# Row statistics by ScalarE's summed squares, in a convolution and expert kernel

## The chip, the cores and the metric

The kernel runs on one core of a Trainium2 chip. The metric is the device time of one execution in microseconds (us). A core has TensorE (matmuls into PSUM), VectorE, ScalarE and GpSimd (elementwise work), and SyncE, whose queue issues most DMA transfers. In the profile they are PE (PEld is its loading of weights), DVE, ACT, POOL and SP. Each runs its instructions in program order and waits on semaphores for the others.

## What is computed

The reference, cut to what matters; S = 2048 rows, D = 512 columns, 8 experts with F = 1792:

```python
def _A_ref(q, k, v, shift_k, ssm_k, ssm_D):
    k_shift = ...                      # causal depthwise convolution of 4 taps
    kv = k_shift * v
    y = irfft2(rfft2(kv_pad) * rfft2(kf_pad))[:S]   # causal convolution over all S rows
    y = y + kv * ssm_D
    return q * y

def _B_ref(x, w_gate, w1, w2):
    logits = xf @ w_gate
    topk_idx = argsort(-logits)[:, :1]
    gates = softmax(topk_val)
    for e in range(E):
        out = out + w * (silu(xf @ w1[e]) @ w2[e])   # w: gate where topk_idx == e, else 0
    ...

x = A_q
h = x + _A_ref(_layernorm(x), A_k, A_v, A_shift_k, A_ssm_k, A_ssm_D)
h2 = h + _B_ref(_layernorm(h), B_w_gate, B_w1, B_w2)
```

The second layer norm needs, for each row of h, its mean and variance over the 512 columns. They are "the second statistics" of this document. The mean does not enter the logits, since the gate's weights have their column means taken out; the variance scales them, which does not move the largest one.

## The kernel before

**Three stages.** The convolution with all that belongs to h; the routing (which row goes to which expert, and a table of rows); the experts, one after the other, with their weights streamed from memory.

**The convolution.** The 2048 rows lie as 128 partitions x 16, and the columns as 4 channels (`c`) of 128. Four of the 16 make a unit (`u`), so a unit is a tile of 128 x 4 x 128, and with four a channel there are 16. For each channel: ScalarE, GpSimd and VectorE make the taps, TensorE turns them (`turn_kv`), VectorE multiplies by v, and stage A (`stage_a`, eight groups of four matmuls for the kernel and eight for kv, into the two `pa` buffers, copied out by ScalarE as `st`) does the first part of a Fourier transform. The second part runs by half channels, eight in all, numbered `i` from 0 to 7: VectorE transposes (`turn`), TensorE multiplies small blocks (`stage_b`, into the one buffer `pb` of four PSUM banks), ScalarE copies (`keep_u`), VectorE multiplies twice (`product1`, `product2`, each after a further block of stage B), TensorE goes back (`back`), and VectorE transposes back (`unturn`, line 350). From one `unturn` to the next is called a period here; the fifth period ends with the fifth of them.

**What belongs to h.** When both halves of a channel are back, each of its four units goes through `last_stage` (TensorE), `gate` (VectorE), `residual` (GpSimd; VectorE for the last channel), which completes h of that unit and channel. Then TensorE turns the unit (`turn_kv` again, line 277), ScalarE copies it (`keep_h`), and for each pair of units TensorE multiplies it with the gate's weights (`logits`) and VectorE adds the result to one sum, `lacc` (`sum_logits`). VectorE also makes the second statistics: `stats` runs four `bn_stats` a unit and channel, and `aggr`, after the last channel, four `bn_aggr` a unit. SyncE stores h (`store_h`). The logits of four channels are summed this way, so that after the last unit one transpose of `lacc` on TensorE gives the routing its logits.

**The order.** The instructions of the convolution are not written in the order of the text. Steps are added to a `Plan` with an engine, a cost and a due time; `Plan.run` picks for each engine the next step, by what is ready and what is due first, and so writes each engine's queue. The due times come from tables (`DK`, `DG`, `DF` and others). PSUM buffers are handed out in turn: `pa` has 2, `pb` 1, `pm` (turned units and logits) 2.

**The routing.** Maximum of the logits, candidates, ranks by a scan and three small matmuls, a table of rows by 16 small matmuls. Then GpSimd gathers the first expert's rows from memory, where h and its four numbers a row (`rec`: mean, root of the variance, two for the gate) were stored.

Of the kernel before, what the change touches and what calls it, by code (L numbers as in the profile page):

```python
# [16 lines left out]
P = 128  # L17
S, D, F, E, KS = 2048, 512, 1792, 8, 4
NJ = S // P
# [112 lines left out]
def kernel(  # L132
# [17 lines left out]
    lacc = keep.tile([P, P], F32, name="lacc")  # L150
    bst2 = keep.tile([P, NJ, ND, 6], F32, name="bst2")
# [28 lines left out]
    ps = conv.enter_context(tc.tile_pool(name="ps", bufs=1, space=PSUM))  # L180
# [8 lines left out]
    GAP = (NU - 1) * E  # L189
    wgc = cp.tile([P, (GAP + E) * ND + GAP], F32, name="wgc")  # L190
    mv1 = cp.tile([P, 2, NJ], F32, name="mv1")
# [185 lines left out]
    def stats(c, u):  # L377
        for i in range(UJ):
            nc.vector.bn_stats(bst2[:, u * UJ + i, c, :], T["h", c, u][:, i, :])

# [3 lines left out]
    def gate_w(c, u):  # L384
        a = (GAP + E) * c + GAP - E * u
        return wgc[:, a:a + NU * E]

    def logits(c, p):
        pl = pt("pm", ("pl", c, p), [P, P])
        for n, u in enumerate((2 * p, 2 * p + 1)):  # L390
            for j in range(UJ):
                nc.tensor.matmul(pl[32 * j:32 * j + 32, :], gate_w(c, u), T["ht", c, u][:, j, :],
                                 start=n == 0, stop=n == 1)

    def sum_logits(c, p):
        if c == 0 and p == 0:
            nc.vector.tensor_copy(lacc, T["pl", c, p])
        else:
            nc.vector.tensor_add(lacc, T["pl", c, p], lacc)

    def aggr(u):
        for j in range(u * UJ, u * UJ + UJ):
            nc.vector.bn_aggr(rec[:, j, 0:2], bst2[:, j, :, :].rearrange("p c s -> p (c s)"))
# [22 lines left out]
    def wg_less():  # L426
        for c in range(ND):
            a = (GAP + E) * c + GAP
            nc.vector.scalar_tensor_tensor(wgc[:, a:a + E], T["pc"], -1.0 / D, wg_sb[:, c, :],
                                           op0=ALU.mult, op1=ALU.add)  # L430

    def casts():
# [5 lines left out]
        nc.gpsimd.tensor_scalar(tok_b, const("tb"), const("ta"), None, op0=ALU.add)  # L438
# [5 lines left out]
    nc.scalar.activation(mv1[:, 0, 0:1], lacc[:, 0:1], AF.Copy)  # L444
    for _ in range(30):
        nc.tensor.matmul(pt("pa", "warm", [P, P]), lacc,
                         lacc, start=True, stop=True)


    DK = (-2.742, -0.93, -7.553, -1.532, -0.994, -6.403)  # L450
    DA = (-0.515, -0.166, -1.312)

    DG = (-7.756, -9.196, -16.731, -2.007, -8.949, -7.899, -12.936, -15.886, 3.939, 2.112)
# [636 lines left out]
```

## Time and profile before

| | |
|---|---|
| three runs | 549.56, 547.93 and 549.28 us; median 549.28 |
| the profiled execution's own time | 549.0 us |
| its span, first to last instruction | 547.1 us |
| PE busy | 521.2 us (95%) |
| DVE busy | 404.2 us (74%) |
| ACT busy | 264.9 us (48%) |
| POOL busy | 262.3 us (48%) |

A busy share is a mean over three stages with different limits, and so the profile is read by stretches. The convolution takes the first 172 us up to its last `unturn` and some 13 more for the last channel's units; the routing starts at about 185 us, the experts' first matmul is at 201 us, and the rest is the experts. The rows of the trace have the start in us from the span's start, the duration, the engine, the line, and the tile that is written with those that are read; in brackets stands how long the engine had been idle and what ended that.

### The profile page before, as it was taken

The numbers are of one execution on the slowest core, as the hardware profiler recorded it, in microseconds if no ns is written. First come the engines' busy times: TensorE is split into PE (matmuls) and PEld (weight loads), VectorE is DVE, ScalarE is ACT, GpSimd is POOL, SyncE is SP. The second block draws the span as 40 slices with busy tenths as digits, with TensorE's granted clock in tenths as the row PEclk, the third lists the DMA queues.
The fourth block names the chain that finished last, engine by engine and source line by source line (L and its number), as shares of the span: only waits on it lengthen the run. The fifth ranks groups of instructions, "written<-read, shape, count | busy, mean of one in ns | idle before, by whom it ended". The sixth has DMA issues, their size and how long they took to land. (4 is left out here: it accounts for less than half of the span.)

```text
span 547.1 us, 12112 instructions
## 1 busy us (share of the span) xinstructions
PE 521.2 (95%) x4800; PEld 451.8 (83%) x4800; DVE 404.2 (74%) x554; ACT 264.9 (48%) x409; POOL 262.3 (48%) x294
## 2 busy tenths in 40 slices
PE   9999989999988699899999999999999999999994
PEld 9867776777646569689999999999988988988973
DVE  3779898999897968857953793884895784784851
ACT  2787886544220336535534444544553553553520
POOL 0555648975550135707703830850770760851831
PEclk9999999999999879999999999999999999999998
DMA  8946586678641269674554555665567467566401
GB/s 282 384 164 199 182 256 180 187 196 281 185 146 40 61 221 350 231 245 144 182 193 155 200 182 161 219 211 181 194 207 253 156 212 247 191 217 204 153 2 40
DMA packets 42452, 105.26 MB, mean 192 GB/s; under 512 B 6464, under 2 KB 14784, under 8 KB 42002
## 3 DMA queue, kind: packets, MB, share of 16 engines
q1 hardware_dynamic: 39602, 95.89, 52.8%
q0 software_dynamic: 2784, 8.51, 4.8%
q8 instruction: 40, 0.66, 0.5%
q14 instruction: 26, 0.21, 0.1%
HBM read 95.96 MB, written 8.47 MB: 191 GB/s over the span
## 5 line engine op out<-in xcount | busy, mean ns | idle before, releaser
L817 POOL TENSOR_TENSOR hl<-s,hh 128x240 fp32r<-128x240 f32 (+5 forms) x112 | 117.2, 1060 | 162.4 <-DVE hh L816 161.8
L798 DVE TENSOR_TENSOR wlo<-raw,whi 128x1024 fp32r<-128x1024 f32 x112 | 159.7, 1439 | 44.7 <-ACT whi L797 44.6
L797 ACT ACTIVATE whi<-raw 128x1024 fp32r<-128x1024 f32 x112 | 114.7, 1052 | 3.9 <-DMA raw<-in_w_dram 3.9
L815 ACT ACTIVATE s<-acc 128x240 f32<-128x240 f32 (+5 forms) x112 | 43.1, 387 | 107.1 <-PE acc L812 67.3
L816 DVE CAST hh<-s 128x240 fp32r<-128x240 f32 (+5 forms) x112 | 55.1, 502 | 37.6 <-ACT s L815 37.4
L812 PE MATMUL acc<-xh,whi 128*128 128x240 f32 (+5 forms) x448 | 72.7, 284 | 0.6 <-ACT xh L773 0.6
L812 PE MATMUL acc<-xl,whi 128*128 128x240 f32 (+5 forms) x448 | 72.0, 283 | 0.0
L812 PE MATMUL acc<-xh,wlo 128*128 128x240 f32 (+5 forms) x448 | 71.9, 283 | 0.0
L812 PEld LDWEIGHTS acc<-xh,whi 128*128 128x128 f32 x448 | 61.7, 189 | 1.3 <-ACT xh L773 0.8
L812 PEld LDWEIGHTS acc<-xl,whi 128*128 128x128 f32 x448 | 61.5, 189 | 0.0
L812 PEld LDWEIGHTS acc<-xh,wlo 128*128 128x128 f32 x448 | 61.4, 189 | 0.0
L832 PE MATMUL acc<-whi,hh 128*128 128x512 f32 (+2 forms) x140 | 55.9, 399 | 0.0
L832 PE MATMUL acc<-whi,hl 128*128 128x512 f32 (+2 forms) x140 | 55.3, 395 | 0.0
L832 PE MATMUL acc<-wlo,hh 128*128 128x512 f32 (+2 forms) x140 | 55.0, 393 | 0.0
L265 POOL TENSOR_TENSOR acc<-acc,ac 128x512 f32<-128x512 f32 x26 | 33.1, 1279 | 37.5 <-ACT acc L253 19.1
L835 PE MATMUL acc<-hh,whi 128*128 128x304 f32 (+2 forms) x168 | 49.8, 296 | 0.0
L835 PE MATMUL acc<-hl,whi 128*128 128x304 f32 (+2 forms) x168 | 49.2, 293 | 0.0
L835 PE MATMUL acc<-hh,wlo 128*128 128x304 f32 (+2 forms) x168 | 49.2, 293 | 0.0
L296 ACT ACTIVATE st<-pa 128x512 f32<-128x512 f32 x64 | 37.3, 595 | 19.7 <-PE pa L293 19.6
L293 PEld LDWEIGHTS pa<-kv,tw 128*128 128x128 f32 x256 | 30.2, 191 | 12.2 <-ACT st L296 8.7
L293 PE MATMUL pa<-kv,tw 128*128 128x128 f32 x256 | 33.5, 282 | 2.2 <-ACT st L296 2.2
L835 PEld LDWEIGHTS acc<-hh,whi 128*128 128x128 f32 x168 | 31.6, 188 | 0.1
(157 smaller groups left out, 848.1 us busy)
## 6 DMA issues: line engine op xcount, KB each, us to landing
raw<-in_w_dram SPq DMA_DIRECT2D x112, 512.0 KB, 4.2
tv<-in_tab_v_dram SPq DMA_DIRECT2D x12, 512.0 KB, 4.5
h<-in_q_dram SPq DMA_DIRECT2D x16, 256.0 KB, 4.4
kt<-in_kt_dram SPq DMA_DIRECT2D x3, 1216.0 KB, 8.1
v<-in_v_dram SPq DMA_DIRECT2D x12, 256.0 KB, 4.4
kern<-in_ssm_dram SPq DMA_DIRECT2D x12, 256.0 KB, 3.4
h<-in_x_dram SPq DMA_DIRECT2D x12, 256.0 KB, 3.9
h_dram<-h SPq DMA_DIRECT2D x12, 256.0 KB, 3.5
```

The source lines that it names most:

```text
L265: nc.gpsimd.tensor_add(T[a, c, u], T[a, c, u], T[b, c, u])
L293: nc.tensor.matmul(p[:, :, j], tw[:, u * UJ + j, r, :], src[:, j, :], start=True, stop=True)
L296: nc.scalar.activation(T["s" + kind, c][:, r * NU + u], T["pa", kind, c, u, r], AF.Copy)
L797: nc.scalar.activation(whi, raw, AF.Copy)
L798: nc.vector.tensor_sub(wlo, raw, whi.bitcast(F32))
L812: nc.tensor.matmul(pu, a[:, k, fs], b[:, k, :], start=i == 0, stop=i == 3 * ND - 1)
L815: nc.scalar.activation(s, pu, AF.Silu)
L816: nc.vector.tensor_copy(hh[:, f, :], s)
L817: nc.gpsimd.tensor_sub(hl[:, f, :], s, hh[:, f, :].bitcast(F32))
L832: nc.tensor.matmul(pd[:ds_.stop - ds_.start], b[:, f, ds_], a[:, f % 2, :], start=f == 0 and i == 0, stop=f == 2 * NCH - 1 and i == 2)
L835: nc.tensor.matmul(pd, a[:, f % 2, ds_], b[:, f, :], start=f == 0 and i == 0, stop=f == 2 * NCH - 1 and i == 2)
```

## The change

Three things change together.

**The second statistics.** `stats` and `aggr` on VectorE go. In their place ScalarE runs `squares`: for each of the four 128x128 slices of a unit one ACTIVATE `Square` of h minus the first norm's mean (its bias, one number a partition), whose sum over the 128 columns goes to `sq`. The sum of h itself comes out of the logits: the gate's weights get a ninth column of ones, and each unit's logits so have nine columns. For that the weights of a channel now have 32 columns, 16 for each unit of a pair, and `lacc` has two halves, one for each pair of units. After the convolution GpSimd adds the four channels of `sq`, divides, and takes the square of the mean's difference off.

**The last unit.** The last unit of the last channel is turned and copied in two halves (`turn_half`, `keep_half`), and its logits don't pass through `lacc`: four matmuls add them in PSUM to the transposed `lacc`.

**The order.** All tables of due times are new, with a table `DE` of its own for the last channel; in the routing a reciprocal, the exponential and the store of `rec` stand later.

The diff, cut to its core:

```diff
-    lacc = keep.tile([P, P], F32, name="lacc")
-    bst2 = keep.tile([P, NJ, ND, 6], F32, name="bst2")
+    lacc = keep.tile([P, 2, P], F32, name="lacc")
+    sq = keep.tile([P, NJ, ND], F32, name="sq")
...
-    wgc = cp.tile([P, (GAP + E) * ND + GAP], F32, name="wgc")
+    wgc = cp.tile([P, 32 * ND + 16], F32, name="wgc")
+    junk = cp.tile([P, P], BF16, name="junk")
...
-    def stats(c, u):
-        for i in range(UJ):
-            nc.vector.bn_stats(bst2[:, u * UJ + i, c, :], T["h", c, u][:, i, :])
...
+    def turn_half(c, u, k):
+        p = pt("pm", ("pht", c, u, k), [P, 2, P])
+        for i in range(2):
+            nc.tensor.transpose(p[:, i, :], T["h", c, u][:, 2 * k + i, :], ident)
+
+    def keep_half(c, u, k):
+        t = T["ht", c, u] if k else sb("ht", ("ht", c, u))
+        nc.scalar.activation(t[:, 2 * k:2 * k + 2], T["pht", c, u, k], AF.Copy)
+
+    def squares(c, u):
+        for i in range(UJ):
+            j = u * UJ + i
+            nc.scalar.activation(junk, T["h", c, u][:, i, :], AF.Square, bias=mv1[:, 0, j:j + 1],
+                                 accum_out=sq[:, j, c:c + 1])
...
-    DF = (2.156, 4.2, -1.718, -7.172, -11.095, -0.093, -7.929, 1.515, -6.905, 5.228, -10.922)
+    DF = (2.33, 3.001, -2.081, -12.063, -6.5, -3.31, -11.581, -4.654, -5.162, 4.313, -35.62)
+    DE = (2.794, -2.565, -5.315, -14.858, -3.123, 1.353, -8.873, -8.482, 0.765, -0.771, -22.145)
...
-            add("DVE", 0.8, o + DF[9], stats, c, u, uses=[("h", c, u)], makes=[(None, ("bs", c, u))])
-            add("SP", 0.26 * MB, o + DF[10], store_h, c, u, uses=[("h", c, u)])
-            if c == ND - 1:
-                add("DVE", 0.6, o + DF[9] + 0.1, aggr, u, uses=[("bs", k, u) for k in range(ND)])
+            add("ACT", 1.2, o + f[9], squares, c, u, uses=[("h", c, u), "mv1"])
+            add("SP", 0.26 * MB, o + f[10], store_h, c, u, uses=[("h", c, u)])
...
-    nc.tensor.transpose(pl, lacc, ident)
+    nc.tensor.matmul(pl[:, 0], lacc[:, 0], ident, start=True, stop=True)
+    nc.tensor.matmul(pl[:, 1], lacc[:, 1], ident, start=True, stop=False)
+    for j in range(UJ):
+        nc.tensor.matmul(pl[:, 1, 32 * j + 16:32 * j + 17 + E], T["ht", ND - 1, NU - 1][:, j, :],
+                         gate_w(ND - 1, 0)[:, :E + 1], start=False, stop=j == UJ - 1)
...
+    nc.scalar.activation(in_j(rec[:, :, 0]), in_t(plj[:, :, E]), AF.Copy, scale=1.0 / D)
+    nc.gpsimd.tensor_add(sq[:, :, 0:2], sq[:, :, 0:2], sq[:, :, 2:4])
+    nc.gpsimd.tensor_add(var, sq[:, :, 0], sq[:, :, 1])
+    nc.gpsimd.tensor_scalar(var, var, 1.0 / D, EPS, op0=ALU.mult, op1=ALU.add)
+    nc.gpsimd.tensor_add(rec[:, :, 1], rec[:, :, 0], mv1[:, 0, :])
+    nc.gpsimd.tensor_mul(rec[:, :, 1], rec[:, :, 1], rec[:, :, 1])
+    nc.gpsimd.tensor_sub(rec[:, :, 1], var, rec[:, :, 1])
```

VectorE in the eighth period, before (L379 is `bn_stats`, L338 and L342 the products, L318 and L350 the transposes, L369 the gate, L399 the logits' sum):

```order
L350 STREAM_TRANSPOSE zs<-pb 128x64x16x2
L369 TENSOR_TENSOR xn<-pa,xn 128x512
L318 STREAM_TRANSPOSE xa<-st 128x2048
L379 BN_STATS bst_63<-h 128x6 x4
L369 TENSOR_TENSOR xn<-pa,xn 128x512
L338 TENSOR_TENSOR p_2087<-pb,xb 128x2048
L379 BN_STATS bst_63<-h 128x6 x4
L399 TENSOR_TENSOR lacc<-pm,lacc 128x128
L379 BN_STATS bst_63<-h 128x6 x4
L342 TENSOR_TENSOR xb<-pb,xb 128x2048
L369 TENSOR_TENSOR xn<-pa,xn 128x512
L350 STREAM_TRANSPOSE zs<-pb 128x64x16x2
```

VectorE in the same period after the change (L320 and L352 the transposes, L340 and L344 the products, L371 the gate, L395 the logits' sum):

```order
L352 STREAM_TRANSPOSE zs<-pb 128x64x16x2
L395 TENSOR_TENSOR lacc<-pm,lacc 128x128
L371 TENSOR_TENSOR xn<-pa,xn 128x512
L320 STREAM_TRANSPOSE xa<-st 128x2048
L371 TENSOR_TENSOR xn<-pa,xn 128x512
L340 TENSOR_TENSOR p_2087<-pb,xb 128x2048
L395 TENSOR_TENSOR lacc<-pm,lacc 128x128
L344 TENSOR_TENSOR xb<-pb,xb 128x2048
L371 TENSOR_TENSOR xn<-pa,xn 128x512
L352 STREAM_TRANSPOSE zs<-pb 128x64x16x2
```

The statistics are gone from between the products; the three gates stand there as they did, and a second sum of logits has come in.

TensorE in the fifth period, before, from its first block of stage B to the way back (L329 is stage B, and the way back where it reads `p`; L365 the last stage, L293 stage A, L277 the turning of a unit):

```order
L329 MATMUL pb<-xa,cb 32x512 x16
L365 MATMUL pa<-zs,tv 128x128 x8
L293 MATMUL pa<-kv,tw 128x128 x4
L329 MATMUL pb<-xb,cb 32x512 x16
L293 MATMUL pa<-kv,tw 128x128 x4
L277 MATMUL pm<-cs,h 128x128 x4
L277 MATMUL pm<-cs,acc 128x128 x4
L293 MATMUL pa<-kern,tw 128x128 x4
L329 MATMUL pb<-xb,cb 32x512 x16
L293 MATMUL pa<-kv,tw 128x128 x8
L277 MATMUL pm<-cs,h 128x128 x4
L329 MATMUL pb<-p_1458,cb 32x512 x16
```

TensorE there after the change (L331 is stage B and the way back, L367 the last stage, L295 stage A, L279 the turning, L390 the logits):

```order
L331 MATMUL pb<-xa,cb 32x512 x16
L295 MATMUL pa<-kv,tw 128x128 x8
L279 MATMUL pm<-cs,acc 128x128 x4
L331 MATMUL pb<-xb,cb 32x512 x16
L279 MATMUL pm<-cs,h 128x128 x4
L367 MATMUL pa<-zs,tv 128x128 x8
L331 MATMUL pb<-xb,cb 32x512 x16
L390 MATMUL pm<-ht,wgc 32x128 x8
L295 MATMUL pa<-kv,tw 128x128 x8
L331 MATMUL pb<-p_1459,cb 32x512 x16
```

A last-stage unit has moved behind the second block, two groups of stage A stand before it together, one group has left the period and a pair's logits have come in.

ScalarE at the end of the convolution, before (L382 copies a turned unit, L615 is the root of the variance):

```order
L382 ACTIVATE ht_2191<-pm_2185 128x512
L382 ACTIVATE ht_2247<-pm_2232 128x512
L382 ACTIVATE ht_2270<-pm_2255 128x512
L382 ACTIVATE ht_2294<-pm_2278 128x512
L382 ACTIVATE ht_2311<-pm_2302 128x512
L615 ACTIVATE rec_64<-rec_64 128x16
```

ScalarE there after the change (L411 are the squares of a unit, L380 and L406 copy a turned unit and a turned half):

```order
L411 ACTIVATE junk_95,sq_63<-st_1642,mv1_64 128x128 x4
L380 ACTIVATE ht_2272<-pm_2257 128x512
L411 ACTIVATE junk_95,sq_63<-st_1642,mv1_64 128x128 x4
L380 ACTIVATE ht_2297<-pm_2290 128x512
L411 ACTIVATE junk_95,sq_63<-st_1642,mv1_64 128x128 x4
L406 ACTIVATE ht_2316<-pm_2309 128x256
L406 ACTIVATE ht_2316<-pm_2313 128x256
L647 ACTIVATE rec_65<-pl_2323 128x2x4x2
L655 ACTIVATE rec_65<-rec_65 128x16
```

A unit's squares stand ahead of the copy of the same turned unit, and those of the last unit ahead of its two halves.

## Rows read from the trace of the kernel before

**Rows 1.** Busy us and instruction count of each engine, by stretch of the span.

```profile
core 0: us, PE busy (x) PEld busy (x) DVE busy (x) ACT busy (x) POOL busy (x), PEclk, DMA share, GB/s
100.00:145.00 45.00, 44.88 (x715) 31.80 (x715) 41.01 (x46) 19.90 (x27) 31.93 (x52) 1.00 0.68 209
145.00:172.00 27.00, 22.64 (x393) 13.54 (x392) 24.34 (x33) 5.46 (x7) 10.89 (x17) 1.00 0.46 135
```

**Rows 2.** Timeline of VectorE: start us, duration, line, tile; L350 is the transpose back.

```profile
103.87 2.32 DVE L350 STREAM_TRANSPOSE zs<-pb 128x2048 f32<-128x2048 f32 x1
...
120.61 2.32 DVE L350 STREAM_TRANSPOSE zs<-pb 128x2048 f32<-128x2048 f32 x1 [0.22 <-PE pb L329]
...
137.36 2.32 DVE L350 STREAM_TRANSPOSE zs<-pb 128x2048 f32<-128x2048 f32 x1 [0.55 <-PE pb L329]
...
153.58 2.32 DVE L350 STREAM_TRANSPOSE zs<-pb 128x2048 f32<-128x2048 f32 x1
...
169.28 2.32 DVE L350 STREAM_TRANSPOSE zs<-pb 128x2048 f32<-128x2048 f32 x1 [1.84 <-PE pb L329]
```

**Rows 3.** Timeline of TensorE in the fifth period; x counts both passes of a matmul.

```profile
106.11 0.60 PE L277 MATMUL pm<-cs,acc 128*128 128x128 f32 x4
106.64 1.14 PE L329 MATMUL pb<-xa,cb 32*32 32x512 f32 x32
107.71 2.09 PE L365 MATMUL pa<-zs,tv 128*128 128x128 f32 x16
109.64 1.05 PE L293 MATMUL pa<-kv,tw 128*128 128x128 f32 x8
...
118.22 1.15 PE L329 MATMUL pb<-p,cb 32*32 32x512 f32 x32
119.10 1.47 PE L329 MATMUL pb<-xa,cb 32*32 32x512 f32 x32
120.50 0.64 PE L392 MATMUL pm<-ht,wgc 128*32 128x128 f32 x16
```

**Rows 4.** Timeline of all engines in the eighth period: the chain through `pb`.

```profile
157.28 1.88 ACT L335 ACTIVATE xb<-pb 128x2048 f32<-128x2048 f32 x1 [6.08 <-PE pb L329]
...
160.61 2.29 DVE L338 TENSOR_TENSOR p<-pb,xb 128x2048 f32<-128x2048 f32 x1 [0.58 <-PE pb L329]
...
162.82 0.86 DVE L379 BATCH_NORM_STATS2 bst<-h 128x6 f32<-128x128 f32 x4
...
162.96 1.15 PE L329 MATMUL pb<-xa,cb 32*32 32x512 f32 x32 [0.29 <-DVE p L338]
...
164.57 2.27 DVE L342 TENSOR_TENSOR xb<-pb,xb 128x2048 f32<-128x2048 f32 x1
```

**Rows 5.** VectorE by line, 20 to 185 us: the statistics of the first three channels.

```profile
L379 DVE BATCH_NORM_STATS2 bst<-h 128x6 f32<-128x128 f32 x48 | 10.3, 277 | 0.6 <-POOL h L372 0.6
```

**Rows 6.** Timeline of TensorE in the third period.

```profile
71.38 3.00 PE L293 MATMUL pa<-kv,tw 128*128 128x128 f32 x24 [1.52 <-ACT st L296]
```

**Rows 7.** Timeline of ScalarE: two taps in a row, and a small copy with a root.

```profile
80.71 0.22 ACT L415 ACTIVATE mv<-mv 128x16 f32<-128x16 f32 x1
...
85.94 1.32 ACT L261 ACTIVATE ac<-kt,shw_sb 128x512 f32<-128x512 f32 x2
```

**Rows 8.** Timeline of VectorE in the tail.

```profile
174.50 0.69 DVE L372 TENSOR_TENSOR st<-st 128x512 f32<-128x512 f32 x1
...
180.83 0.69 DVE L372 TENSOR_TENSOR st<-st 128x512 f32<-128x512 f32 x1
...
184.15 0.27 DVE L399 TENSOR_TENSOR lacc<-pm,lacc 128x128 f32<-128x128 f32 x1
...
185.06 0.29 DVE L621 TENSOR_REDUCE mx<-pl 128x16 f32<-128x128 f32 x1
```

**Rows 9.** Timeline of SyncE's queue and of GpSimd: statistics stored, rows gathered.

```profile
187.76 0.61 SPq L649 DMA_DIRECT2D h_dram<-rec  x1
...
194.35 1.20 POOL L707 DMA_INDIRECT first<-h_dram,idxg  x1 [3.22 <-DVE wide_i L697]
```

More of the change, by code (lines that the diff above doesn't have):

```diff
@@ L384, in gate_w, with logits, sum_logits @@
     def gate_w(c, u):
[L385 to L390, printed above, removed]
+        a = 32 * c + 16 - 16 * (u % 2)
+        return wgc[:, a:a + 32]
+    def logits(c, us):
+        pl = pt("pm", ("pl", c, us[-1]), [P, P])
+        for u in us:
             for j in range(UJ):
                 nc.tensor.matmul(pl[32 * j:32 * j + 32, :], gate_w(c, u), T["ht", c, u][:, j, :],
[L393 to L397, printed above, removed]
-        else:
[L399 to L403, printed above, removed]
+                                 start=u == us[0], stop=u == us[-1])
+    def sum_logits(c, u):
+        if c:
+            nc.vector.tensor_add(lacc[:, u // 2], T["pl", c, u], lacc[:, u // 2])
+        else:
+            nc.vector.tensor_copy(lacc[:, u // 2], T["pl", c, u])
+    def turn_half(c, u, k):
[10 more added lines that the diff above has]
+                                 accum_out=sq[:, j, c:c + 1])
     def stats1(j):
@@ L595 @@
[L595 to L597 removed]
+            if (c, u) != LAST:
+                add("PE", 0.45, o + f[5], turn_kv, ("h", c, u), ("pht", c, u), uses=[("h", c, u)],
+                    makes=[("pm", ("pht", c, u))])
+                add("ACT", 0.62, o + f[6], keep_h, c, u, uses=[("pht", c, u)], makes=[("ht", ("ht", c, u))])
+                us = (u,) if (c, u) == (LAST[0], LAST[1] - 1) else (u - 1, u)
+                if u % 2 or len(us) == 1:
+                    add("PE", 0.2 + 0.27 * len(us), o + f[7], logits, c, us, uses=[("ht", c, k) for k in us] + ["wgc"],
+                        makes=[("pm", ("pl", c, u))])
+                    add("DVE", 0.28, o + f[8], sum_logits, c, u, uses=[("pl", c, u)] + ([("lg", u // 2)] if c else []),
+                        makes=[] if c else [(None, ("lg", u // 2))])
+            else:
+                for k in range(2):
+                    add("PE", 0.25, o + f[5], turn_half, c, u, k, uses=[("h", c, u)], makes=[("pm", ("pht", c, u, k))])
+                    add("ACT", 0.38, o + f[6], keep_half, c, u, k, uses=[("pht", c, u, k)],
+                        **(dict(puts=[("ht", c, u)]) if k else dict(makes=[("ht", ("ht", c, u))])))
@@ L640 @@
                                  oh.rearrange("p e j -> p (e j)"), 0.0, op0=ALU.mult, op1=ALU.add)
+    nc.vector.reciprocal(rec[:, :, 1], rec[:, :, 1])
+    nc.gpsimd.tensor_mul(top, top, rec[:, :, 1])
+    nc.scalar.activation(rec[:, :, 3], top, AF.Exp)
     pn = ps_t.tile([P, E], F32, name="pn")
@@ L669 @@
                                    op0=ALU.mult, op1=ALU.add)
+    nc.vector.reciprocal(rec[:, :, 2], rec[:, :, 3])
+    nc.gpsimd.tensor_mul(rec[:, :, 2], rec[:, :, 2], rec[:, :, 3])
+    nc.sync.dma_start(h_rows[:, :, D:RW], rec)
     nc.vector.tensor_tensor(r2, r2, oh, op=ALU.mult)
```

86 lines of the change are left out of this document (39 added, 47 removed).

## The prediction

> **What bounds the kernel now.** I read the busy times by stretch first [rows 1]. From 100 to 145 us TensorE is busy 44.88 of 45.00 us, and VectorE 41.01: both are full. From 145 to 172 us TensorE falls to 22.64 of 27, VectorE stays at 24.34, and ScalarE has work for 5.46. So up to 145 us TensorE sets the pace, and after that a chain that runs through VectorE. GpSimd and ScalarE have time to spare in both stretches.
>
> Then the convolution's period. Each of the eight half channels ends with one transpose back on VectorE (L350). The last five start at 103.87, 120.61, 137.36, 153.58 and 169.28 [rows 2], so the fifth to eighth periods last 16.74, 16.75, 16.22 and 15.70 us.
>
> What is a period made of? TensorE's pieces, from start to start [rows 3]: a block of stage B 1.07 us, a last-stage unit 1.93, turning a unit about 0.5, a group of four stage-A matmuls about 1.0, a logits pair 0.6, the way back 0.88 + 1.47, say 2.3. Counted from the order of before, the fifth period holds 3 blocks, the way back, 2 last-stage units, 5 turns and 5 groups: 3.2 + 2.3 + 3.9 + 2.5 + 5.0 = 16.9, against 16.74 measured. The sixth gives 17.1 against 16.75. Here TensorE is the bound. The seventh gives 14.6 against 16.22, the eighth 13.0 against 15.70: there it is not.
>
> In those two the chain through the one buffer `pb` is the bound [rows 4]: stage B, ScalarE's copy (157.28, 1.88 us), stage B, first product (160.61, 2.29), stage B (162.96), second product (164.57), the way back, transpose. TensorE's block that feeds the second product ends at 162.96 + 1.15 = 164.11, but the product starts at 164.57, behind row statistics that began at 162.82 and more behind them. So 0.46 us of the eighth period are the statistics', and the chain alone takes 15.70 - 0.46 = 15.24 us. That is a floor for every period.
>
> **The change, part by part.** All terms count against the profiled execution's own 549.0 us; the three plain runs have 549.28 as their median, 0.05% above.
>
> *VectorE's statistics go.* 48 `bn_stats` of 0.277 us [rows 5] leave the periods from the fourth to the last, 16 more and 16 aggregations leave the tail. That is 10.3 us of VectorE before 172 us, but it is worth only what the chain waits for.
>
> *The order.* By the order after the change the fifth period has one turn and one group less and one logits pair more: 3.2 + 2.3 + 3.9 + 2.0 + 4.0 + 0.6 = 16.0 us; the sixth one group less and half a us of others: 16.4. The seventh has 15.0 and the eighth 14.1 of TensorE's time, under the floor. So the work has been spread: less where TensorE is the bound, more where it has idle time. I take 16.0, 16.4, 15.5 (floor, and two pieces that TensorE does before a block of the chain) and 15.35: gains of 0.7, 0.35, 0.7 and 0.35, in sum **2.1**. Bounds: 0, if new waits fill what is freed, and 4.45, if all four fall to 15.24.
>
> *The third period's stall.* At 71.38 TensorE had waited 1.52 us for ScalarE [rows 6], which was in its long copy while both stage-A buffers were full. In the new order only two stage-A groups stand before the next block of stage B, not three. The stall itself may stay, but the block comes sooner. I take **0.5**; the ends are 0 and 1.5.
>
> *The price of the squares.* No row of before shows a sum written out by ScalarE. Nearest is a tap of the convolution, also from SBUF with an operand of one number per partition: two of 128x512 take 1.32 us [rows 7]. A root of 128x16 takes 0.22 and a copy of 128x2048 1.88 [rows 4, 7], so an element costs 0.00082 us; 384 fewer of them make 0.40 us for a single 128x128 square and 0.29 when it follows another. Four in a row: 1.27 us, the lower end. At the upper end every sum is written out by one more small instruction at the 0.22 of the smallest row with nothing overlapped: 4 x (0.40 + 0.22), about 2.4. I take 1.67: the write-out costs 0.10 behind its square, since neighbours on ScalarE overlap by 0.1. The Trainium skill (ScalarE: Activation LUTs, What ACT_TABLE_LOAD costs) gives 280 ns and 0.833 ns an element with a pointer operand, and 93 ns of overlap; by it two taps take 1.32 us, as the row has it, four squares without a write-out 1.27 us, and the sum would be 0.4 us lower than mine.
>
> Sixteen such units are 27 us of ScalarE, from the fourth period to the tail. It has 25.1 us idle between 100 and 145 and 21.5 between 145 and 172 [rows 1], so they fit; what each unit displaces is the next question. ScalarE works in order: a unit of squares waits for GpSimd's residual, and behind it stand the copy of the turned unit, copies out of stage A and, once in each of the last four periods, the long copy of the chain. I put no cost on it in the middle value: by the order after the change, TensorE turns that same unit, which also needs the residual, with one to five us of its own work ahead of the block that the long copy waits for.
>
> *The tail.* Now: the last residual starts at 180.83, the last logits sum at 184.15, behind statistics and aggregations, and the routing's first maximum at 185.06 [rows 8]. After: a logits sum (0.25) goes in ahead of the last residual, which so ends at 181.77; ScalarE does u (a unit of squares) and then two half copies (0.42 + 0.31), TensorE its last small matmuls and hand-overs (0.65): the maximum starts at 183.15 + u. But ScalarE also has all four units of squares of the last channel after the residual that ends at 174.50 + 0.69 [rows 8], with three copies of 0.5 between and the same end: 178.1 + 4u. With u = 1.67 these are 184.8 and 184.8: a gain of **0.2**. With 1.27 it is 0.6; with 2.4 it is a loss of 2.6. From 1.74 on the tail loses.
>
> *Routing.* One reciprocal leaves the way to the candidates and one enters it after the ranks: zero. Root, exponential and table loads stand beside the scan and the counting. The row statistics go to memory some 1.3 us later than the 187.76 of now, and GpSimd's gather reads them at 194.35 [rows 9]: over 5 us are left, so zero; if the store took longer than that, it would cost the rest. The experts' stage is unchanged and follows its first gather: it moves as a whole.
>
> Sum: 549.0 - 2.1 - 0.5 - 0.2 = **546.2 us**.
>
> **Rivals.** *All periods at the floor.* For it: VectorE, which stood in the chain with its statistics, has 10 us less to do. Against: TensorE's own work in the fifth and sixth period is over 15.24. 549.0 - 4.45 - 0.5 - 0.2 = 543.9.
>
> *The freed time buys nothing.* TensorE was full until 145 us and stays so; the new pieces ahead of the chain's blocks (turns that wait for residuals, logits that wait for copies behind the squares) take what the statistics gave. For it: 16.9 and 17.1 are TensorE's own sums, not VectorE's. Then only the tail remains: 548.8, no change.
>
> *The squares are dear and ScalarE holds the chain.* This is the case that ends slower. The place is the long copy behind a unit of squares, in the last four periods, and the tail. If a unit takes 2.4 us and the block of stage B ends while one is running, the copy waits half a unit, 1.2 us, four times; the tail loses 2.6: 549.0 - 2.6 + 4.8 + 2.6 = 553.8. It decides from about 1.9 us a unit if they collide in every period, and from 2.8 in the tail alone. For it: the unknown write-out, and ScalarE's order. Against: ScalarE's idle time, and the work of TensorE that stands between a residual and the block. The Trainium skill (ScalarE: Activation LUTs, Rules for kernel authors) wants such arithmetic on VectorE, which by it does an element up to three times faster in bf16; the trace, in fp32, agrees on the price (0.277 against 0.29 and more), but VectorE is the engine without time. *Between*, with 2.0 to 2.3 us a unit and no collisions, tail and periods cancel: 548.5.
>
> **Chances.** 0.3% of the time is 1.65 us, about what a measurement can tell from no change. My forecast 0.50, with its own range of 545.0 to 547.6; the floor 0.13; nothing bought 0.14; between 0.11; dear 0.12. Faster: 0.50 but for a small part, and the floor: 0.61. Same: 0.27. Slower: 0.12. The range runs from 543.7 to 550.0 and leaves out the dear squares and a little below.
>
> **What would show it.** Right: periods of about 16.0, 16.4, 15.5 and 15.3 between the transposes back; no VectorE row between stage B's end and a product; a unit of squares at 1.3 to 1.9 us; the first maximum 13.2 us after the last transpose ends, as against 13.5 now; from there to GpSimd's gather the same 9.3 us. Wrong: ScalarE's long copy starting over 0.5 us after its block, squares of 2 us and more, TensorE waiting for turned units, or a gather that waits for the store of the statistics.

## The result: slower by 1.1%, and the profile after

The changed kernel takes 555.19 us (median of 4 runs, 553.43 to 555.64) against 548.61 for the kernel before (4 runs, 547.55 to 549.56): a ratio of 1.0109 with an interval of 1.0074 to 1.0144. Forecast were 546.2, and a range that ended at 550.0. The profiled execution after is the 553.43, the shortest of the four, with a span of 551.5 us against 547.1. So the stages below take apart 4.4 of the 6.6 us between the medians; the other 2.2 lie in executions of which there is no trace. Stage by stage, in us of the two spans:

| stretch | before | after | difference | forecast |
|---|---|---|---|---|
| start to the first transpose back | 43.77 | 43.97 | +0.20 | 0 |
| second period | 18.15 | 17.62 | -0.53 | 0 |
| third | 23.44 | 24.50 | +1.06 | -0.5 |
| fourth | 18.51 | 17.77 | -0.74 | 0 |
| fifth, sixth, seventh | 49.71 | 48.49 | -1.22 | -1.75 |
| eighth | 15.70 | 16.84 | +1.14 | -0.35 |
| tail: end of the last transpose back to the first maximum | 13.46 | 16.71 | +3.25 | -0.2 |
| first maximum to GpSimd's gather | 9.29 | 11.03 | +1.74 | 0 |
| gather to the experts' first matmul | 6.90 | 6.93 | +0.03 | 0 |
| experts | 345.85 | 345.32 | -0.53 | 0 |

The transposes back, where [rows 2] has those of before:

```profile
103.86 2.32 DVE L352 STREAM_TRANSPOSE zs<-pb 128x2048 f32<-128x2048 f32 x1
120.32 2.32 DVE L352 STREAM_TRANSPOSE zs<-pb 128x2048 f32<-128x2048 f32 x1
136.54 2.32 DVE L352 STREAM_TRANSPOSE zs<-pb 128x2048 f32<-128x2048 f32 x1
152.35 2.28 DVE L352 STREAM_TRANSPOSE zs<-pb 128x2048 f32<-128x2048 f32 x1
169.19 2.32 DVE L352 STREAM_TRANSPOSE zs<-pb 128x2048 f32<-128x2048 f32 x1 [1.84 <-PE pb L331]
```

At 152.35 the changed kernel is 1.23 us ahead of before; at 169.19 it is level. What took that is one turning of a unit on TensorE (L279), ahead of the chain's block (L331) that feeds the second product. It waits for GpSimd (POOL), which comes to that unit's residual (L374) only at 160.65:

```profile
159.47 0.66 PE L279 MATMUL pm<-cs,h 128*128 128x128 f32 x4
161.97 0.66 PE L279 MATMUL pm<-cs,h 128*128 128x128 f32 x4 [1.85 <-POOL h L374]
162.56 0.64 PE L390 MATMUL pm<-ht,wgc 128*32 128x128 f32 x16
163.13 1.16 PE L331 MATMUL pb<-xa,cb 32*32 32x512 f32 x32
...
159.78 2.29 DVE L340 TENSOR_TENSOR p<-pb,xb 128x2048 f32<-128x2048 f32 x1 [0.72 <-PE pb L331]
...
159.81 0.88 POOL L360 TENSOR_SCALAR st<-st,mv 128x128 f32<-128x128 f32 x2
160.65 1.27 POOL L374 TENSOR_TENSOR h<-h,xn 128x512 f32<-128x512 f32 x1
```

The first product (L340) ends at 159.78 + 2.29 = 162.07, so the block could have started there; it starts at 163.13.

The third period. TensorE waits at the place of [rows 6], and now for 2.16 us instead of 1.52; behind it the granted clock is half. First the row, then the stretches (the number before the last two is the clock, 1.00 the full 2.4 GHz, 0.50 the 1.2):

```profile
71.41 3.31 PE L295 MATMUL pa<-kv,tw 128*128 128x128 f32 x16 [2.16 <-ACT st L298]
...
72.00:74.00 2.00, 2.00 (x12) 2.00 (x11) 1.93 (x6) 1.05 (x2) 0.00 (x0) 0.50 0.81 305
74.00:76.00 2.00, 2.00 (x36) 0.70 (x34) 0.83 (x3) 1.24 (x3) 0.00 (x0) 0.66 0.80 246
```

Before, the clock is 1.00 in both stretches.

The tail, where [rows 8] has VectorE before. ScalarE's first unit of squares with the copy behind it, the end of its line, TensorE's last matmuls and the maximum:

```profile
175.39 0.40 ACT L411 ACTIVATE junk<-st,mv 128x128 bf16<-128x128 f32 x1 [4.04 <-DVE st L374]
175.70 0.19 ACT L411 ACTIVATION_READ_ACCUMULATOR junk<-st,mv 128x1 f32 x1
175.92 0.40 ACT L411 ACTIVATE junk<-st,mv 128x128 bf16<-128x128 f32 x1
...
177.37 0.58 ACT L380 ACTIVATE ht<-pm 128x512 f32<-128x512 f32 x1
...
184.71 0.64 ACT L406 ACTIVATE ht<-pm 128x256 f32<-128x256 f32 x2
...
185.40 0.80 PE L634 MATMUL pl<-cs,lacc 128*128 128x128 f32 x2 [1.23 <-ACT ht L406]
185.99 0.63 PE L635 MATMUL pl<-cs,lacc 128*128 128x128 f32 x2
186.41 1.72 PE L637 MATMUL pl<-wgc,ht 128*128 128x9 f32 x8
...
188.22 0.29 DVE L646 TENSOR_REDUCE mx<-pl 128x16 f32<-128x128 f32 x1 [4.54 <-PE pl L637]
```

Each sum is written out by an instruction of its own, and a unit goes from 175.39 to 177.37: 1.98 us. From 175.39 to 184.71 ScalarE does not pause. From its last copy's end (184.71 + 0.64 = 185.35) to the maximum pass 2.87 us, at half clock (0.50 from 185.0 us on). Before, the last copy and the transpose behind it were:

```profile
182.39 0.60 ACT L382 ACTIVATE ht<-pm 128x512 f32<-128x512 f32 x1 [0.81 <-PE pm L277]
...
184.48 0.48 PE L618 MATMUL pl<-cs,lacc 128*128 128x128 f32 x1 [1.01 <-DVE lacc L399]
```

That copy ends at 182.99, and from there to the maximum (185.06) pass 2.07 us, also at half clock from 184.5 on. Counted from the end of the last transpose back, the last copy ends after 13.84 us, before after 11.39. So of the tail's 3.25 us, 2.45 lie ahead of the last copy's end and 0.80 behind it.

Routing, where [rows 9] has before: the store, VectorE's last reduction and the gather:

```profile
192.48 0.61 SPq L702 DMA_DIRECT2D h_dram<-rec  x1
...
197.56 0.16 DVE L730 TENSOR_REDUCE wide_i<-nover 1x2 int32<-1x16 f32 x1
...
199.25 1.20 POOL L740 DMA_INDIRECT first<-h_dram,idxg  x1 [4.75 <-issue]
```

The store leaves 4.26 us after the maximum, before 2.70. The gather starts 1.53 us after VectorE is through; before, it followed at once (194.19 + 0.16, 194.35).

### The profile page after: what moved, and what is told of

The parts are those of the page before. It is cut to its first block, busy times and chain, and to the rows that moved or that the text cites. A ratio compares the mean times of both kernels' runs of the same rounds, so it can differ in the third digit from the quotient of the medians.

```text
span 551.5 us, 12184 instructions
## 1 busy us (share of the span) xinstructions
PE 525.1 (95%) x4803; PEld 455.4 (83%) x4803; DVE 390.3 (71%) x474; ACT 293.3 (53%) x539; POOL 262.6 (48%) x300
## 5 line engine op out<-in xcount | busy, mean ns | idle before, releaser
L831 DVE TENSOR_TENSOR wlo<-raw,whi 128x1024 fp32r<-128x1024 f32 x112 | 158.0, 1423 | 46.1 <-ACT whi L830 45.9
L849 DVE CAST hh<-s 128x240 fp32r<-128x240 f32 (+5 forms) x112 | 56.6, 514 | 37.5 <-ACT s L848 37.3
L295 PEld LDWEIGHTS pa<-kv,tw 128*128 128x128 f32 x256 | 31.3, 198 | 11.6 <-ACT st L298 6.0
L295 PE MATMUL pa<-kv,tw 128*128 128x128 f32 x256 | 34.5, 288 | 2.8 <-ACT st L298 2.8
```

The lines of the kernel that those rows point to most:

```text
L295: nc.tensor.matmul(p[:, :, j], tw[:, u * UJ + j, r, :], src[:, j, :], start=True, stop=True)
L831: nc.vector.tensor_sub(wlo, raw, whi.bitcast(F32))
L849: nc.vector.tensor_copy(hh[:, f, :], s)
```

## The experiments

Each kernel ran beside runs of the kernel before on the same chip: the first four rows below beside one set of them, the next four beside a second, the last two beside a third. Across sets only the ratios compare. "First to eighth" is from the first transpose back to the eighth in the profile (before 125.51), "tail" as above (13.46), "store" and "gather" count from the first maximum (2.70 and 9.29).

| kernel | ratio to before, 95% | first to eighth | third | eighth | tail | store | gather |
|---|---|---|---|---|---|---|---|
| after_again | 1.0133 (1.0095 to 1.0170) | 126.19 | 24.59 | 18.20 | 18.44 | 4.24 | 10.65 |
| no_squares | 1.0028 (1.0005 to 1.0050) | 124.36 | 24.51 | 16.74 | 14.40 | 4.25 | 10.94 |
| store_early | 1.0131 (1.0107 to 1.0154) | 130.10 | 24.50 | 18.13 | 16.76 | - | 9.49 |
| turn_later | 1.0061 (1.0040 to 1.0082) | 124.06 | 24.52 | 15.83 | 16.71 | 4.25 | 11.26 |
| squares_no_sum | 1.0029 (0.9999 to 1.0060) | 124.58 | 24.53 | 16.99 | 14.30 | 4.25 | 11.08 |
| stall_filled | 1.0067 (1.0039 to 1.0095) | 123.73 | 22.96 | 16.86 | 16.71 | 4.25 | 10.32 |
| old_order | 1.0095 (1.0062 to 1.0129) | 124.95 | 23.42 | 15.44 | 16.95 | 4.25 | 10.63 |
| whole_last | 1.0036 (1.0003 to 1.0070) | 123.88 | 22.97 | 17.17 | 13.90 | 4.42 | 11.20 |
| before_no_stats | 0.9973 (0.9949 to 0.9997) | 123.99 | 23.43 | 15.44 | 13.46 | 2.70 | 9.29 |
| mended | 0.9945 (0.9923 to 0.9966) | 122.28 | 22.96 | 15.83 | 13.18 | 3.55 | 10.51 |

**after_again**, no edit.

> The changed kernel once more, as it is, to stand beside the others of this call. Against the kernel before it should again be 4 to 7 us longer (1.0109 with an interval of 1.0074 to 1.0144 in the first comparison). In its profile I look at four places: the clock between 71 and 76 us (half in the first profile, after 2.16 us in which TensorE waited), the eighth period (16.84 us from the start of the seventh transpose back to that of the eighth, before the change 15.70), the tail from the end of the last transpose back to the routing's first maximum (16.7 us, before 13.5) and from there to GpSimd's gather (11.0 us, before 9.3). If these four are the loss, all four come again. If the fallen clock at 71 us was chance, it is away here and the time is 1 to 2 us less.

All four places came again, and two were worse: the eighth period 18.20 and the tail 18.44. The same turn waited 2.22 us here, and the clock fell behind it:

```profile
161.47 0.66 PE L279 MATMUL pm<-cs,h 128*128 128x128 f32 x4 [2.22 <-POOL h L374]
162.06 0.65 PE L390 MATMUL pm<-ht,wgc 128*32 128x128 f32 x16
162.63 2.03 PE L331 MATMUL pb<-xa,cb 32*32 32x512 f32 x32
...
164.00:166.00 2.00, 2.00 (x22) 1.41 (x7) 1.20 (x1) 0.01 (x1) 0.00 (x0) 0.50 0.04 7
```

The block that takes 1.16 us at full clock takes 2.03. In this run the clock also fell at 172 us, after a wait of 1.58 us. That plain runs of the changed kernel take up to 2 us more than its first profiled execution would fit such falls; it is shown for this one alone, since plain runs leave no trace.

**no_squares**.

```diff
     def squares(c, u):
-        for i in range(UJ):
...
+        pass
```

> The changed kernel with no squares at all: the sums of squares are set to a constant, so the variance of the second norm isn't computed. Order and everything else are the same. Theory 1, ScalarE's line of squares makes the tail: a unit of four takes 2.36 us where I had put 1.67, and four units with their copies stand one behind the other. Then the tail falls from 16.7 to about 12.5 us (TensorE's last units and the halves then set it), and the time by 3.5 to 4.5 us. Theory 2, it is the order on TensorE (logits and turns ahead of what is waited for): the tail falls by under 1.5 us. For the periods before: if ScalarE's squares also hold the chain, the eighth period falls from 16.84 to under 16.2 too; if that is the order's, it stays within 0.3.

The tail falls by 2.3 us, less than theory 1 said and more than theory 2; the eighth period stays at 16.74, so ScalarE does not hold the chain there. What the tail still has over that of before, 0.9 us, is 0.7 ahead of the last copy's end (12.08 us behind the transpose back, before 11.39) and 0.2 behind it (2.31 against 2.07, again at half clock). The expectation's 2.36 us a unit add up durations that overlap; from start to start a unit is 1.98.

**store_early**.

```diff
+        if (c, u) == (1, 0):
+            nc.gpsimd.memset(rec0, 1.0)
+            nc.sync.dma_start(h_rows[:, :, D:RW], rec0)
...
-    nc.sync.dma_start(h_rows[:, :, D:RW], rec)
```

> The changed kernel, with the 32 KB store of rec left out of the routing and the store of a constant of the same form made at about 100 us in its place: the gathered rows carry constants instead of mean, deviation and probability. Theory: GpSimd's gather waits for that store, which is issued 4.26 us after the first maximum (2.70 before the change) and takes about 6.7 us to land. Then the gather follows the last reduction of VectorE (197.7) instead of starting at 199.25: 1.5 us less, and from first maximum to gather about 9.5 us instead of 11.0. Rival: the gather waits for something else that came late (GpSimd's own queue, its indices): no change, within 0.3 us.

The gather follows VectorE's last reduction (201.78) at once, as the theory had it:

```profile
201.94 1.21 POOL L743 DMA_INDIRECT first<-h_dram,idxg  x1 [3.22 <-DVE wide_i L733]
```

The time is not shorter than that of after_again (1.0131 against 1.0133), for a reason that I had not thought of: the moved store, 2048 pieces of 16 bytes, went out at 104.82 ahead of a load of `h` issued at 106.66, which GpSimd got only at 114.80 after 4.19 us of waiting (in the changed kernel issued at 107.77, there by 111.98). TensorE then waited 2.57 us for a residual, the clock fell to half, and the sixth period took 20.31 us. In the eighth it fell too, behind a wait of 1.91 us: 18.13.

**turn_later**.

```diff
-                add("PE", 0.45, o + f[5], turn_kv, ...
+                add("PE", 0.45, o + f[5] + 13.1 * ((c, u) == (2, 2)), turn_kv, ...
```

> The changed kernel with one piece moved on TensorE alone: the turning of the third unit of the third channel, which stood in the eighth period ahead of the chain's third block of stage B and waited 1.85 us there for GpSimd's residual, comes behind that block and a last-stage unit. No other engine's order changes. Theory, that turn holds the chain: the block starts at about 162.1 instead of 163.1, the eighth period falls from 16.84 to 15.8 to 16.1, and the time by 0.7 to 1.0 us. Rival, VectorE or the logits hold the second product anyway, or the tail, which is ScalarE's, takes back what the period gives: the time moves by less than 0.3 us.

```profile
161.74 1.15 PE L331 MATMUL pb<-xa,cb 32*32 32x512 f32 x32
162.82 2.08 PE L367 MATMUL pa<-zs,tv 128*128 128x128 f32 x16
164.74 0.60 PE L279 MATMUL pm<-cs,h 128*128 128x128 f32 x4
165.41 1.15 PE L331 MATMUL pb<-p,cb 32*32 32x512 f32 x32
```

The turn now waits for nothing, and the eighth period is 15.83: one piece moved, 1.0 us of the period. The median fell by 3.2 us against after_again (552.50 from 555.74), more than the period; this fits a clock that has no such wait to fall in any more, but plain runs don't show it.

**squares_no_sum**.

```diff
-            nc.scalar.activation(junk, T["h", c, u][:, i, :], AF.Square, bias=mv1[:, 0, j:j + 1],
-                                 accum_out=sq[:, j, c:c + 1])
+            nc.scalar.activation(junk, T["h", c, u][:, i, :], AF.Square, bias=mv1[:, 0, j:j + 1])
```

> The changed kernel with the squares left in place but their sums not written out (the variance of the second norm isn't computed; a constant stands for it). In the profile each sum written out is an instruction of its own, 0.19 us on the record, and a unit takes 1.98 us from its first square to the copy behind it. Theory 1, the write-outs are what made a unit dearer than the row of two taps told: a unit falls to about 1.3 us; the four units with their copies (4 x 1.8 us) then keep pace with TensorE's 2.25 us a unit, only the last unit's squares stand ahead of the half copies, and the tail falls from 16.7 to 14.8 to 15.6 us; the time falls by 1 to 2 us. Rival, the write-outs lie beside the squares and cost nothing: a unit stays over 1.8 us and the tail within 0.3 us of 16.7.

```profile
174.40 1.70 ACT L411 ACTIVATE junk<-st,mv 128x128 bf16<-128x128 f32 x4 [4.22 <-DVE st L374]
176.01 0.58 ACT L380 ACTIVATE ht<-pm 128x512 f32<-128x512 f32 x1
```

A unit falls only to 1.61 us, not 1.3: four squares of 0.40 span 1.70, so they start every 0.43, and a sum written out adds 0.09 to each ((1.98 - 1.61) / 4). The tail falls by 2.4, more than forecast and as much as without any squares. Of that, 1.2 are ScalarE's line from the first square to the half copies (8.08 us instead of 9.32; with 1.61 + 0.48 a unit it all but keeps pace with TensorE's 2.25). Another 1.0 lies behind the last copy (1.89 us to the maximum instead of 2.87), where the clock is still full when the last matmuls begin, and 0.2 ahead of the first square.

**stall_filled**.

```diff
             nc.tensor.transpose(p[:, i, :], T[src][:, i, :], ident)
+        if key == ("pkv", 2, 1):
+            for j in range(2 * UJ):
+                nc.tensor.matmul(T["pa", "k", 2, 2, 1][:, :, j % UJ], ...)
```

> The changed kernel with eight matmuls of a stage-A group repeated, into the same PSUM tile with the same result, at the place of the third period where TensorE waits 2.2 to 2.7 us for ScalarE's long copy. Nothing else is moved. In every profile of the changed kernel so far the clock granted after that wait was half for 3 to 4 us; in that of the kernel before, which waited 1.52 us there, it stayed full. Theory, the wait brings the clock down, and that is the third period's loss: the clock stays at 1.0 from 70 to 76 us, the third period falls from 24.5 to 23.0 to 23.5 us and the time by 1.0 to 1.5 us. Rival, the period is set by ScalarE's copies, whatever the clock: it stays over 24.2 us and the time does not move by more than 0.4 us.

```profile
70.00:72.00 2.00, 1.63 (x15) 1.44 (x14) 2.00 (x2) 1.85 (x5) 1.25 (x1) 1.00 0.76 216
72.00:74.00 2.00, 2.00 (x41) 1.04 (x40) 1.93 (x5) 1.70 (x4) 0.00 (x0) 1.00 0.80 287
74.00:76.00 2.00, 2.00 (x19) 2.00 (x20) 1.97 (x3) 1.66 (x4) 1.28 (x1) 1.00 0.72 249
```

The clock stays full and the third period is 22.96: the fallen clock cost 1.5 us, and without it the new order is 0.5 us faster there than before, as forecast. One profile, whole_last, had the wait (2.16 us) and kept the clock, with 22.97: the period follows the clock, not ScalarE. The ratio is 1.0067, where the changed kernel had 1.0109 and 1.0133 in other sets: more than the period gives, as with turn_later, and no trace shows where.

**old_order**.

```diff
-    DK = (-2.046, -0.781, -9.547, -0.847, 0.151, -10.04)
+    DK = (-2.742, -0.93, -7.553, -1.532, -0.994, -6.403)
...
+    DE = DF
```

> The edits alone: squares, ninth column and halves as in the changed kernel, but with the due times of before (one table for all channels). On TensorE the order is that of before but for the eighth period and the tail. Theory, the order took what the statistics gave: the third period is 23.4 us again with the clock at full, the fifth to seventh are 16.7, 16.7 and 16.0 or a little less, the tail stays long (16 to 17 us), the gather waits for the store; about 2.5 to 4 us over the kernel before and 1.5 to 3 us under the changed one. Rival, the new order is the good part and the squares the bad one: then this is no faster than the changed kernel, 555 us or more.

The third period is that of before and the tail is as long as with the new order: the tail belongs to the edits, not to the order. In all it is 1.0095, 5 us over before where 2.5 to 4 were expected, which the intervals don't tell from the changed kernel. From first to eighth transpose it gains 0.56 us on before, where leaving out the statistics alone, by the same tables, gains 1.52 (before_no_stats): the edits take 1 us back. They do so in the sixth and seventh periods (17.04 and 16.79, expected 16.7 and 16.0). In the seventh, unlike what the expectation says, TensorE's order is not that of before: a turn stands ahead of a last-stage unit and the chain's block and waits 0.47 us for GpSimd. In the sixth, three groups of stage A take 3.29 us instead of 3.00 while two copies out of stage A stand behind a unit of squares on ScalarE; that this is the cause is argued, not tried. The second period is 18.03, near the 18.15 of before, against 17.1 to 17.6 in every kernel with the new tables: its gain is the order's.

**whole_last**.

```diff
-            if (c, u) != LAST:
+            if True:
...
-        nc.tensor.matmul(pl[:, 1, 32 * j + 16:32 * j + 17 + E], T["ht", ND - 1, NU - 1][:, j, :],
-                         gate_w(ND - 1, 0)[:, :E + 1], start=False, stop=j == UJ - 1)
...
-            add("ACT", 1.2, o + f[9], squares, c, u, ...
+            add("ACT", 1.2, o + f[9] + 16.0 * ((c, u) == LAST), squares, c, u, ...
```

> The changed kernel with the last unit taken whole, as before: turned and copied in one piece, its logits through lacc with those of its neighbour, two plain transposes at the end, and its squares behind its copy on ScalarE. Order before the tail as in the changed kernel. Theory, half of the tail's loss is the way of the halves: their last matmuls take 2.3 to 2.9 us from the last copy to the maximum where I had put 0.65, and the copies stand behind the last squares. Then the tail falls from 16.7 to 13.2 to 14.0 us; the store of rec comes up to 0.7 us later after the maximum; the time falls by 2.2 to 3.2 us. Rival, ScalarE's line of three other units of squares holds the last copy all the same: the tail stays over 15.5 us.

```profile
180.11 1.06 ACT L380 ACTIVATE ht<-pm 128x512 f32<-128x512 f32 x2
...
180.74 0.91 PE L390 MATMUL pm<-ht,wgc 128*32 128x128 f32 x16 [0.29 <-ACT ht L380]
182.06 0.66 PE L629 MATMUL pl<-cs,lacc 128*128 128x128 f32 x2 [0.41 <-DVE lacc L395]
182.51 0.64 PE L630 MATMUL pl<-cs,lacc 128*128 128x128 f32 x2
...
183.24 0.29 DVE L638 TENSOR_REDUCE mx<-pl 128x16 f32<-128x128 f32 x1 [1.23 <-PE pl L630]
```

The tail falls by 2.8 us to 13.90, with as many squares. Two things changed at once: the last unit's squares now stand behind the last copy, and its logits go the old way. The rows part them. The last copy ends at 181.17, 11.82 us behind the transpose back instead of 13.84: 2.0 us, a unit of squares. From there to the maximum pass 2.07 us instead of 2.87, exactly as before the change: 0.8 us. So the larger part of this gain is the place of the last squares, not the way of the halves; no run changed one without the other.

**before_no_stats**, the kernel before without the statistics of three channels.

```diff
-        for i in range(UJ):
+        for i in range(UJ) if c == ND - 1 else ():
             nc.vector.bn_stats(bst2[:, u * UJ + i, c, :], T["h", c, u][:, i, :])
```

> The kernel before, with its own order on every engine, only without the bn_stats of the first three channels (48 instructions, 10.3 us of VectorE between 78 and 170 us); constants stand in their place, so the second norm's variance isn't computed. The last channel keeps its statistics, the tail is unchanged. This is the price of the statistics by themselves. Theory, they lay beside other work nearly everywhere: from the first transpose back to the eighth 125.5 us become 124.5 to 125.2, by the 0.46 us of the eighth period and little more, and the time falls by 0.3 to 1.0 us. Rival, VectorE with 41 of 45 us busy was as much the bound as TensorE: each period falls by over half a us and the time by 2 us or more.

10.3 us of VectorE are worth 1.52 us from first to eighth transpose: 0.81 in the fourth period, 0 in the fifth, 0 in the sixth, 0.37 in the seventh and 0.26 in the eighth. The fourth I had not priced; the eighth I had at 0.46. The rival (2 us or more) falls, and so does my upper bound of 1.0. In the eighth, stage B's block and the second product are now

```profile
160.91 1.15 PE L329 MATMUL pb<-xa,cb 32*32 32x512 f32 x32 [0.40 <-DVE p L338]
...
162.23 2.29 DVE L342 TENSOR_TENSOR xb<-pb,xb 128x2048 f32<-128x2048 f32 x1 [1.19 <-PE pb L329]
```

and the product, with nothing ahead of it on VectorE, still starts 0.17 us behind the block's end (162.06). So not all of the 0.46 was the statistics': the hand-over itself stays, and the chain alone takes 15.44 us, not 15.24.

**mended**, from the changed kernel with turn_later, stall_filled, whole_last and this (both reciprocals and the store of `rec` also stand earlier in the routing):

```diff
-            nc.scalar.activation(junk, T["h", c, u][:, i, :], AF.Square, bias=mv1[:, 0, j:j + 1],
+            nc.scalar.activation(junk, T["h", c, u][:, i, :], AF.Square,
...
+    nc.scalar.activation(in_j(rec[:, :, 1]), in_t(plj[:, :, E]), AF.Square, scale=1.0 / D)
...
-    nc.gpsimd.tensor_add(rec[:, :, 1], rec[:, :, 0], mv1[:, 0, :])
-    nc.gpsimd.tensor_mul(rec[:, :, 1], rec[:, :, 1], rec[:, :, 1])
```

> The changed kernel with what the runs before pointed to, put together: the turn of the third unit behind the chain's block in the eighth period, the third period's wait filled with eight repeated matmuls, the last unit whole, and in the routing a shorter way to the store of rec: squares of h itself without the first mean, so that the mean's square comes from ScalarE out of PSUM in place of two GpSimd steps, and both reciprocals earlier on VectorE. By the parts measured so far: from the first transpose back to the eighth 122.5 us (17.3, 23.0, 17.8, 16.5, 16.2, 15.8, 15.9; before 125.5), the tail 13.9, store 3.6 us after the maximum, gather 10.3 after it. The first expert's matmul at 199.5 instead of 201.25 and about 545 us of span: 1 to 3 us faster than the kernel before. Rival, the gains in the periods are taken back, by clock that falls in other waits or in the tail: no difference from the kernel before, within 0.3%.

546.75 us (12 runs) against 549.73: 0.55% faster than before, with an interval of 0.9923 to 0.9966.

```profile
171.79 0.31 ACT L415 ACTIVATE junk<-st 128x128 bf16<-128x128 f32 x1 [4.21 <-DVE st L378]
172.00 0.19 ACT L415 ACTIVATION_READ_ACCUMULATOR junk<-st 128x1 f32 x1
...
181.27 0.29 DVE L642 TENSOR_REDUCE mx<-pl 128x16 f32<-128x128 f32 x1 [0.86 <-PE pl L634]
...
184.82 0.61 SPq L682 DMA_DIRECT2D h_dram<-rec  x1
...
199.29 0.71 PE L839 MATMUL acc<-xh,whi 128*128 128x240 f32 x4 [0.63 <-ACT xh L800]
```

The stages came as added up, and the experts start at 199.29 instead of the 201.25 of before. In this tail the clock stays full, and from the last copy's end to the maximum pass 1.69 us. A square without an operand of one number per partition takes 0.31 us instead of 0.40, which I had not expected.

## Why the prediction was wrong, step by step

The profiled execution lies 4.4 us over before, where I had put 2.8 under. Of these 7.2 us the tail is 3.45, the way to the gather 1.74, the third period 1.56, the eighth 1.49 and the fifth to seventh 0.53; 1.27 in the second and fourth periods, on which I had put nothing, and 0.3 elsewhere go the other way.

**The tail: two terms were too small.** Of my formula 178.1 + 4u, first u: the price by the taps [rows 7] let each square begin 0.1 us before its neighbour's end. Without write-outs squares of 0.40 us follow each other every 0.43, with no overlap, and the write-out adds 0.09, where I had 0.10: 1.98 us, not 1.67. (The `bn_stats` of such a slice took VectorE 0.277 [rows 5]; my 0.29 for a square was an estimate, and too low.) The Trainium skill (ScalarE: Activation LUTs, What ACT_TABLE_LOAD costs) has neighbours on ScalarE overlap by 93 ns; the copy behind the squares agrees (0.58 us on the record, 0.48 to the next start), the squares, which all write one tile, do not, so the measurement decides. Whether the shared tile is the cause wasn't tried. On the line of four units that is 1.1 us (9.32 us measured from first square to half copies, 8.18 by the formula). By itself that would have made the tail lose 1 us. Second, and larger, "last small matmuls and hand-overs 0.65": measured 2.87 us, of which four 128x9 matmuls with the turned unit as weights (x8 in the row, two passes each) take 1.72 alone, with the clock fallen to half in the wait of 1.23 ahead of the last matmuls. The 0.65 was a guess with no row: before, the same way takes 2.07 us with VectorE's statistics in it, and 2.07 in whole_last without them. So the halves and their matmuls added 0.8; the rest of the miss in this term was in the kernel before and I had not looked. 1.1 + 2.2, with 0.1 of other small differences, are the miss of 3.4 us (188.22 against 184.8).

The two terms stand in one line, and no run takes out one of them alone: squares_no_sum shortens ScalarE's line by 1.2 us and what follows by 1.0, whole_last the line by 2.0 and what follows by 0.8. Against the kernel before, the larger part of the tail's loss (2.45 of 3.25) is that ScalarE's last copy comes later, with the last unit's squares ahead of it.

**The store: the slack was never shown.** I set 5 us against the store of `rec` and called it zero. From store to gather pass 6.77 us here and 6.1 to 7.0 in the profiles where the gather waits for it; before, 6.59 passed too, and I read the time up to the gather as slack, when nothing showed that the store had landed earlier. I also had the store 1.3 us later in absolute time, when the whole tail was 3.2 us later as well: relative to the maximum it is 1.56 us later, and the gather loses 1.53. My own sentence "if the store took longer than that, it would cost the rest" was the right mechanism, with no chance set on it.

**The periods: a collision that I put at nothing, and gains where I had none.** Fifth to seventh gained 1.22 of 1.75. turn_later with stall_filled's third period, as mended has both, gives 122.28 us from first to eighth transpose, 3.2 under before, where I had 2.6. That this comes near is luck: 1.4 of the 3.2 lie in the second and fourth periods, and the four that I had priced gain 1.4 instead of 2.1. The fourth period's gain is the statistics' (0.81 in before_no_stats), the second's the order's (old_order). The eighth lost its gain to one turn that stands ahead of the chain's block and waits for GpSimd: this is the rival "the freed time buys nothing" in its mechanism, for one period. I had taken from the order that TensorE has 14.1 us of work there and put that under the floor; a sum of work does not tell that a piece ahead of the block waits. turn_later takes 1.0 us of it back; of the 0.5 that it stays over my 15.35, 0.2 are the floor that I had too low.

**The third period: the wait was half seen.** I read the stall of 1.52 us and said that the block comes sooner. It would; but the new order also moves a group of stage A from behind the block of stage B whose long copy ScalarE is making to ahead of it, so less is left to do while ScalarE copies, the wait is 2.16 us, and the clock falls behind it. With the clock full (stall_filled, whole_last) the gain of 0.5 is there. In [rows 6] nothing points to that: the clock stayed at 1.00 there.

**The rivals.** "The squares are dear and ScalarE holds the chain" had 553.8, near the profiled 553.43, but that is luck: of its 4.8 us of collisions the runs show about 0.25. In the eighth period ScalarE has been idle for 2.23 us when the long copy starts, 0.19 us behind its block's end (156.26), and no_squares leaves that period as it is. In the fifth the copy starts 0.58 us behind its block's end (107.78), with ScalarE busy without a pause since a unit's squares began at 104.67; without squares it is 0.31, and the fifth period is 16.21 instead of 16.46. That is the rival's mechanism, and one of my signs of being wrong, in one period of four.

```profile
155.12 1.14 PE L331 MATMUL pb<-xb,cb 32*32 32x512 f32 x32
...
156.45 1.88 ACT L337 ACTIVATE xb<-pb 128x2048 f32<-128x2048 f32 x1 [2.23 <-PE pb L331]
...
106.64 1.14 PE L331 MATMUL pb<-xa,cb 32*32 32x512 f32 x32
...
108.36 1.86 ACT L337 ACTIVATE xa<-pb 128x2048 f32<-128x2048 f32 x1
```

Of its price the tail came near, with a loss of 3.25 us for its 2.6, but by its formula the measured unit of squares makes only 1 us of that. *Between* had the unit nearly right (2.0 to 2.3 us) and the time, 548.5, too low: it has the same 0.65, and nothing for the store and the waits of TensorE. "All periods at the floor" falls: no period of any run reached the floor of 15.24; the shortest is the eighth of old_order and before_no_stats with 15.44.

## What to carry to other kernels

A sum of work per engine bounds a period from below; what a new order costs is found by asking, for each piece that now stands ahead of a block of the chain, what that piece waits for and whether it has come. A term of the last hand-overs needs rows too, above all when its instructions are new in shape. What an engine need not have done before its last copy belongs behind that copy. Time that passes between a store and its reader is no slack unless a row shows the store landed. On TensorE a wait costs twice where the clock falls behind it: look for every wait that grows, not only for those that end on the chain.

## What the runs showed of the hardware

- A wait of TensorE of 2.15 to 2.17 us in the third period was followed by half clock for 3 to 4 us in six profiles out of seven; one of 1.52 us at the same place (the kernel before, before_no_stats, old_order) by full clock. In the eighth period 1.91 and 2.22 us were followed by half clock, 1.76, 1.85, 1.87, 2.00 and 2.18 by full. The wait's length alone does not tell it.
- A sum that ScalarE writes out is an instruction of its own: 0.19 us on the record, and it makes a unit of four squares longer by 0.09 for each. A square of 128x128 takes 0.40 us with a bias of one number per partition and 0.31 without; the Trainium skill (ScalarE: Activation LUTs, What ACT_TABLE_LOAD costs) puts 93 ns on such an operand, and the runs agree.
- A store of 2048 pieces of 16 bytes keeps its reader waiting 6.1 to 7.0 us from its issue, and in the one run that put it ahead of loads a 256 KB load issued 1.84 us behind it on the same queue came after 8.1 us instead of 4.2.
